# One transformer block with its gradients on one core: where the second layout of the MLP activation is made, how w2's gradient is laid out for its store, and who issues two small loads

## The chip, the cores and the metric

The kernel runs on one NeuronCore of a Trainium2 chip. The metric is the time of one execution in microseconds of device time; three executions of the kernel before were timed and their median is quoted. One more look, the profile, comes from a single profiled execution. Engine names as in the profile: PE (matrix products; PEld is its weight load), DVE (vector), ACT (scalar/activation), POOL (GpSimd), SP (issues transfers). Transfers are issued by SP, ACT or POOL and carried out by sixteen DMA engines.

## The reference

One decode step of a pre-layernorm block and all its gradients, in bfloat16, batch 2, one query position, width 640, 32 heads of 128, a cache of 4096 positions, MLP width 1728:

```
h   = x + attention(layernorm(x), k_cache, v_cache, wq, wo)     # 32 heads, 4096 keys each
h2  = h + relu(layernorm(h) @ w1) @ w2                          # 640 -> 1728 -> 640
out = h2, and for grad_out: the gradients of x, k_cache, v_cache, wq, wo, w1, w2
```

The caches are 67 MB each (2 x 32 x 4096 x 128 in two bytes), and so are their two gradients. The gradient of w2 is an outer product: for each of 1728 rows f and 640 columns d, the sum over the two batch items of relu(h1)[b, f] * grad_out[b, d]. It is output 7, 1728 x 640. The gradient of w1 is output 6, those of wo and wq outputs 5 and 4.

## The kernel before

**Stages.** The 64 pairs of batch item and head are handled twice. Phase 1 (`p1_iter`) loads the pair's K and V tiles (1 MB each), computes scores, softmax and the quantities for the output. Phase 2 (`p2_iter`) needs the gradient that comes back through the MLP and wo, reads V again where it was not kept (`Wt`, 53 loads), and stores the pair's gradients of K and V (`gK`, `gV`, 1 MB each, issued by POOL, lines 856 and 875). Between them, for each batch item, `middle_gen` (line 719) does the attention output, the second layernorm, the MLP, and the gradient back to the heads. Phase 2 of batch item 0 runs beside phase 1 of item 1.

**Order.** The order is written by hand. The plan loop (line 1116) walks the iterations, and after each piece of an iteration gives a share of steps to three lists of background generators: `bg` (middle_gen and what follows it, `mlp_out` last), `bg2` (`fin_gen`, line 933: the weight gradients) and `bg3` (`gx_gen`, the gradient of x). A generator yields a number that says how much of the share the step used, so taking out or adding steps moves everything the generator emits later against the main iterations. Each engine carries out what it is given in this order.

**Buffers.** The big tiles come from rings of buffers with the tags `ld` (loads), `g` (gK, gV), `f` (weight gradients) and `q`. A ring's buffer is free again when its last reader is through, which for a stored tile is when the store has landed. At the start of `fin_gen` ring `f` has one buffer (line 1145). Eight banks of PSUM are given out by role; the role `mid` has one bank, used by all small products.

**The MLP activation in two layouts.** relu(layernorm(h) @ w1) is wanted with the 1728 rows on partitions. `acol` has row c*128+p in partition p, place c (13 full places and one of 64 rows, NF = 14). For item 1, `middle_gen` also makes `arow`, which has row p*13+c in partition p, place c: lines 751 to 760, 65 products that take w1 as weights with every 13th column, then two small DVE copies. `arow` is read only by `mlp_out` (line 691), whose w2 tiles are loaded so that each partition's rows lie together in memory.

**The row form.** `rows_of` (line 882) turns a column form into rows: `ar` has the activation as a row of 1728 per batch item, in partitions q and q+1 for q = 0, 32, 64, 96; `gr` has grad_out likewise.

**w2's gradient.** `fin_gen` calls `outer_rows` (line 903) for it with cc = 1728 // 96 = 18, so that P = 96 partitions are used and partition p has rows p*18 to p*18+17. Six places go into one tile (`ot`): 6 x 2 products of depth two (512 and 128 columns), each followed by an ACT copy from PSUM to the tile (line 928), then one store issued by ACT (line 930). There are three such tiles, 720 KB each. The same function makes the other weight gradients with 128 partitions.

**The small loads.** x and grad_out (2.5 KB each) are the first two transfers that SP issues (lines 210, 211); the five tiles of wq (1 MB each, line 378) and then K and V tiles follow on the same queue.

Of the kernel before, what the change touches and what calls it, by code (L numbers as in the profile page):

```python
# [7 lines left out]
FP32 = mybir.dt.float32  # L8
# [7 lines left out]
def kernel(  # L16
# [56 lines left out]
    def pst(shape, dtype, role, name):  # L73

        k = banks[role].pop(0)
        banks[role].append(k)
        return ps.tile(shape, dtype, tag=f"bank{k}", bufs=1, name=name)
# [36 lines left out]
    def rested(tag, n):  # L114

        return free[tag] > 0 and (forced[0] or step[0] >= given_at.get(homes[tag][0], -n) + n)
# [90 lines left out]
    nc.vector.memset(acol[:], 0.0)  # L207
    nc.vector.memset(ghfc[:], 0.0)

    nc.sync.dma_start(out=xr[0:2 * ND, :], in_=A_x.rearrange("b s (c p) -> (b s c) p", p=128))  # L210
    nc.sync.dma_start(out=xr[2 * ND:4 * ND, :], in_=grad_out.rearrange("b s (c p) -> (b s c) p", p=128))


    def colsum(src, n):
# [504 lines left out]
    def middle_gen(b):  # L719
        if o_next[0] < (b + 1) * H // OG:  # L720
            o_group()
        nc.vector.tensor_reduce(out=u4[:], in_=u_bank[0][:].rearrange("p (s d) -> p d s", s=4),
                                axis=AX.X, op=ALU.add)
        yield
        while a_next[0] < (b + 1) * H // OG:
            if a_next[0] == o_next[0]:
                o_group()
                yield
                yield
            a_group()  # L730
            yield
        at_bf = small.tile([128, ND], BF16, tag="at_bf", bufs=1, name="at_bf")
        nc.vector.tensor_copy(out=at_bf[:], in_=asum[:, b, :])
        nc.vector.tensor_tensor(out=h1c[:, :, b], in0=xg32[:, b, :], in1=at_bf[:], op=ALU.add)
        h32 = small.tile([128, 1, ND], FP32, tag="h32", bufs=1, name="h32")
        nc.vector.tensor_copy(out=h32[:, 0, :], in_=h1c[:, :, b])
        yield ("a", b)
        u_out(b)
        yield from ln_fwd(h32[:], 1, x2c[:, :, b:b + 1], rstd2[:, b:b + 1])
        hf_ps = pst([128, NF], FP32, "mid", "hf_ps")  # L740
        for cf in range(NF):
            kc = f_kc(cf)
            for c in range(ND):
                nc.tensor.matmul(hf_ps[0:kc, cf:cf + 1], lhsT=w1_t[:, c, cf * 128:cf * 128 + kc],
                                 rhs=x2c[:, c, b:b + 1], start=(c == 0), stop=(c == ND - 1))
            yield 0.25
        nc.vector.tensor_scalar(out=acol[:, 0:NFF, b], in0=hf_ps[:, 0:NFF], scalar1=0.0, scalar2=None, op0=ALU.max)
        if F_rem:
            nc.vector.tensor_scalar(out=acol[0:F_rem, NFF, b:b + 1], in0=hf_ps[0:F_rem, NFF:NF],
                                    scalar1=0.0, scalar2=None, op0=ALU.max)  # L750
        if b == B - 1:
            ar_ps = pst([128, NFF, B], FP32, "mid", "ar_ps")
            for cf in range(NFF):
                for c in range(ND):
                    nc.tensor.matmul(ar_ps[:, cf, :], lhsT=w1_t[:, c, bass.ds(cf, 128, step=NFF)],
                                     rhs=x2c[:, c, :], start=(c == 0), stop=(c == ND - 1))
                yield 0.25
            nc.vector.tensor_scalar(out=arow[:, 0:NFF, :], in0=ar_ps[:], scalar1=0.0, scalar2=None, op0=ALU.max)
            if F_rem:
                nc.vector.tensor_copy(out=arow[:, NFF, :], in_=acol[:, NFF, :])  # L760
        mask = small.tile([128, NF], FP32, tag="mask", bufs=1, name="mask")
        nc.vector.tensor_single_scalar(out=mask[:], in_=acol[:, :, b], scalar=0.0, op=ALU.is_gt)
        nc.vector.tensor_tensor(out=ghfc[:, :, b], in0=ga[:, b, :], in1=mask[:], op=ALU.mult)
        yield from wait(3)
        fbc = cols.tile([128, Dff], BF16, tag="fbc", name="fbc")
        gx2 = small.tile([128, 1, ND], FP32, tag="gx2", bufs=1, name="gx2")
        gx2p = small.tile([128, ND, 3], FP32, tag="gx2p", bufs=1, name="gx2p")
        FW = Dff // 3
        spread_f = bcast_cols(one(ghfc, b), NF, f_kc, fbc)
        have = 0  # L770
        for k in range(3):
            while have < min(Dff, (k + 1) * FW):
                next(spread_f)
                have += 512
                yield
            for c in range(ND):
                yield from turn()
                ttr(w1_t[:, c, k * FW:(k + 1) * FW], fbc[:, k * FW:(k + 1) * FW], gx2p[:, c, k:k + 1], FW)
                yield 0.85
        nc.vector.reduce_sum(out=gx2[:, 0, :], in_=gx2p[:], axis=AX.X)  # L780
        yield ("w1", b)
        yield from ln_bwd(gx2[:], x2c[:, :, b:b + 1], rstd2[:, b:b + 1], gc[:, :, b:b + 1], gh1c[:, :, b:b + 1], 1)
        hbc = cols.tile([128, D], BF16, tag="rowbc", name="hbc")
        yield from bcast_cols(one(gh1c, b), ND, lambda c: 128, hbc)
        yield ("gh1", b)

        first = H - KEPT[b]
        bounds = [(first, first + 2), (first + 2, H)] if b == 0 else [(first, H)]
        bounds += [(h, min(first, h + GH)) for h in range(0, first, GH)]
        for h0, h1 in bounds:  # L790
            yield from go_group(b, h0, h1, hbc)
        if b > 0:
            yield from mlp_out()
# [106 lines left out]

    late = [False]

    def outer_rows(L, nrow, R, N, out_ap, cc):


        P = nrow // cc
        grp = max(1, min(cc, 4096 // N))
        out_v = out_ap.rearrange("(p c) n -> p c n", c=cc)
        for c0 in range(0, cc, grp):
            gn = min(grp, cc - c0)  # L910
            while not rested("f", 13):
                yield 0.0
            ot = take("f", [128, grp, N], "ot")
            todo = [(k, n0, min(512, N - n0)) for k in range(gn) for n0 in range(0, N, 512)]
            made = []
            for x in range(len(todo) + 1):
                if x < len(todo):
                    k, n0, nn = todo[x]
                    q = 32 * (fw[0] % 4)
                    o_ps = pst([128, 512], FP32, "o", "o_ps")  # L920
                    fw[0] += 1
                    nc.tensor.matmul(o_ps[0:P, 0:nn], lhsT=L[q:q + B, bass.ds(c0 + k, P, step=cc)],  # L922
                                     rhs=R[q:q + B, n0:n0 + nn], start=True, stop=True)
                    made.append((o_ps, k, n0, nn))
                    yield 0.3
                if x > 0:
                    o_ps, k, n0, nn = made[x - 1]
                    nc.scalar.copy(out=ot[0:P, k, n0:n0 + nn], in_=o_ps[0:P, 0:nn])  # L928
                    yield 0.3
            nc.scalar.dma_start(out=out_v[:, c0:c0 + gn, :], in_=ot[0:P, 0:gn, :])  # L930
            give(ot)

    def fin_gen(fin):
        FIN["wide"] = [fin.tile([128, 4, 4, 32], BF16, tag="wide", bufs=2, name="wide") for _ in range(2)]
        for w in FIN["wide"]:
            nc.vector.memset(w[:], 0.0)
        yield from wait(2)
        yield from rows_of(fin, acol, NF, "ar", "rX")
        yield from rows_of(fin, gc, ND, "gr", "rD")
        yield from outer_rows(FIN["ar"], Dff, FIN["gr"], D, out_7, Dff // 96)  # L940
        yield from rows_of(fin, ghfc, NF, "ghfr", "rX")
        yield from rows_of(fin, x2c, ND, "x2r", "rD")
        yield from outer_rows(FIN["x2r"], D, FIN["ghfr"], Dff, out_6, ND)
        HH = H // 2
        while ("gh1", B - 1) not in done:
            yield
        yield from rows_of(fin, gh1c, ND, "gh1r", "rD")
        for s0 in range(0, H, HH):
            yield from rows_of(fin, OFc[:, s0:s0 + HH, :], HH, "OFr", "rX")
            yield from outer_rows(FIN["OFr"], HH * 128, FIN["gh1r"], D, out_5[s0 * 128:(s0 + HH) * 128, :], HH)  # L950
        yield from rows_of(fin, x1c, ND, "x1r", "rD")
        for s0 in range(0, H, HH):
            while not all(("go", B - 1, h) in done for h in range(s0, s0 + HH)):
                yield
            yield from rows_of(fin, GQc[:, s0:s0 + HH, :], HH, "GQr", "rX")
            yield from outer_rows(FIN["x1r"], D, FIN["GQr"], HH * 128, out_4[:, s0 * 128:(s0 + HH) * 128], ND)
# [277 lines left out]
```

## Time and profile before

| what | value |
|---|---|
| time, three runs | 910.86, 903.35, 911.38 us; median 910.86 |
| span of the profiled execution | 905.5 us; no time of its own is given beside the span |
| busy: PE, DVE, ACT, POOL | 742.8, 696.1, 444.7, 192.4 us |
| moved by the DMA engines | 362.87 MB, mean 401 GB/s |
| the 65 products for arow (line 755) | from 499.3 to 506.8 us |
| first and last store of a weight gradient issued by ACT (line 930) | 583.7 and 870.8 us |

How to read it: the span runs from the first to the last instruction of the profiled execution. A busy time is the sum over an engine's instructions, and engines work side by side, so busy times do not add up to the span. The views split the span into windows and give, for each, the busy time of each engine with the number of instructions in brackets, the clock that was granted to PE (1.00 is full), the share of the sixteen DMA engines that was busy (1.00 is all of them all the time; pipelining lets it go slightly above) and the rate they moved.

### The profile page before, as it was taken

The numbers are of one execution on the slowest core, as the hardware profiler recorded it, in microseconds if no ns is written. First come the engines' busy times: TensorE is split into PE (matmuls) and PEld (weight loads), VectorE is DVE, ScalarE is ACT, GpSimd is POOL, SyncE is SP. The second block draws the span as 40 slices with busy tenths as digits, with TensorE's granted clock in tenths as the row PEclk, the third lists the DMA queues.
The fourth block names the chain that finished last, engine by engine and source line by source line (L and its number), as shares of the span: only waits on it lengthen the run. The fifth ranks groups of instructions, "written<-read, shape, count | busy, mean of one in ns | idle before, by whom it ended". The sixth has DMA issues, their size and how long they took to land.

```text
span 905.5 us, 24516 instructions
## 1 busy us (share of the span) xinstructions
PE 742.8 (82%) x10205; PEld 620.3 (68%) x10205; DVE 696.1 (77%) x1286; ACT 444.7 (49%) x1096; POOL 192.4 (21%) x330
## 2 busy tenths in 40 slices
PE   3999899899998997987968854877899879859880
PEld 3887788788887887876857744655667656645560
DVE  2666787777888796777869698986898349989982
ACT  1444343344554564554543434644576656637750
POOL 1344433443211110010011111211122111111120
PEclk9999999999999899999885776655555555555655
DMA  8999999999879999999999999999999999999997
GB/s 361 420 409 403 409 398 410 420 417 388 335 306 377 377 406 425 421 424 421 411 398 392 411 423 394 423 398 396 407 401 388 426 420 423 419 423 416 419 421 296
DMA packets 56254, 362.87 MB, mean 401 GB/s; under 512 B 5680, under 2 KB 11696, under 8 KB 15312
## 3 DMA queue, kind: packets, MB, share of 16 engines
q1 hardware_dynamic: 34704, 212.18, 58.1%
q0 software_dynamic: 18432, 134.23, 35.9%
q10 hardware_dynamic: 3008, 14.91, 4.2%
q8 instruction: 80, 1.31, 0.6%
q14 instruction: 30, 0.25, 0.1%
HBM read 212.16 MB, written 149.13 MB: 399 GB/s over the span
## 4 chain that ended last, share of the span: by engine, by line
PE 42%; DMA 25%; DVE 18%; issue 6%; ACT 6%; SPq 1%; POOL 0%; POOLq 0%; ACTq 0%; DVEq 0%
PE t_ps L423 18%; DMA Vt<-in_A_v_cache_dram 13%; PE m_ps L457 9%; DVE gV L818 5%; DMA out_dram<-gV 4%; DVE gK L818 4%; DMA out_dram<-gK 3%; PE s_ps L436 3%; ACT t_sb L428 3%; DMA wqs<-in_A_wq_dram 3%; DVE gxj L644 2%; PE u_ps L486 2%; PE o_ps L922 2%; PE dp_ps L436 2%; DVE pk L464 2%
## 5 line engine op out<-in xcount | busy, mean ns | idle before, releaser
L428 ACT COPY t_sb<-t_ps 128x512 f32<-128x512 f32 x479 | 274.4, 586 | 214.6 <-PE t_ps L423 208.9
L436 PEld LDWEIGHTS <-t_sb 128*128 128x128 bf16 x4096 | 179.0, 102 | 47.0 <-issue 18.8
L423 PE MATMUL t_ps<-ident_f,Wt 128*128 128x128 f32 x848 | 196.5, 379 | 0.2 <-ACT t_sb L428 0.2
L457 PE MATMUL m_ps<-pk,Vt 128*128 128x129 bf16 x2048 | 171.0, 222 | 19.5 <-DMA Vt<-in_A_v_cache_dram 18.2
L464 DVE TENSOR_TENSOR pk<-Kt,ep 128x2048 bf16<-128x2048 bf16 x128 | 156.5, 1223 | 33.9 <-PE m_ps L457 15.8
L818 DVE TENSOR_TENSOR gK<-rb,gsp 128x2048 bf16<-128x2048 bf16 x128 | 152.4, 1225 | 18.4 <-DMA out_dram<-gV 16.4
L818 DVE TENSOR_TENSOR gV<-rb,pp 128x2048 bf16<-128x2048 bf16 x128 | 153.0, 1219 | 15.1 <-DMA out_dram<-gK 12.5
L423 PE MATMUL t_ps<-ident_f,Kt 128*128 128x128 f32 x1024 | 155.1, 284 | 6.6 <-DMA Kt<-in_A_k_cache_dram 6.3
L423 PEld LDWEIGHTS t_ps<-ident_f,Wt 128*128 128x128 f32 x848 | 135.7, 196 | 35.1 <-issue 29.3
L457 PEld LDWEIGHTS <-Vt 128*128 128x128 bf16 x2048 | 124.5, 98 | 51.0 <-issue 29.7
L423 PEld LDWEIGHTS t_ps<-ident_f,Kt 128*128 128x128 f32 x1024 | 112.6, 144 | 10.9 <-PE s_ps L436 4.6
L474 POOL COPY pk<-ep 128x16 bf16<-128x16 bf16 x80 | 83.2, 1042 | 163.6 <-ACT ep L512 87.8
L436 PE MATMUL dp_ps<-gom,t_sb 128*128 128x2 bf16 x2048 | 95.6, 168 | 8.5 <-ACT t_sb L428 7.5
L875 POOL DMA_DIRECT2D out_dram<-gV x64 | 34.2, 534 | 268.0 <-DVE gV L818 207.7
L856 POOL DMA_DIRECT2D out_dram<-gK x64 | 34.0, 532 | 264.9 <-DVE gK L818 207.8
L436 PE MATMUL s_ps<-qm,t_sb 128*128 128x2 bf16 x2048 | 87.4, 164 | 1.5 <-DVE t_sb L426 1.5
L928 ACT CAST ot<-o_ps 128x512 bf16<-128x512 f32 (+4 forms) x160 | 70.4, 490 | 14.8 <-DMA out_dram<-ot 11.2
L571 ACT CAST MT<-m_ps 128x128 bf16<-128x128 f32 x64 | 17.1, 267 | 104.3 <-PE m_ps L457 104.2
L845 ACT ACTIVATE rb<-dp_ps,rt 128x256 bf16<-128x256 f32 x64 | 30.3, 474 | 69.4 <-PE dp_ps L840 68.7
L644 DVE CUSTOM_DVE_ANT_0 junk<-wo_t,hbc 128x640 bf16<-128x640 bf16 x64 | 52.4, 819 | 0.2
L644 DVE CUSTOM_DVE_ANT_0 gxj<-wqs,gqr 128x1024 bf16<-128x1024 bf16 x40 | 48.8, 1221 | 2.4 <-DMA wqs<-in_A_wq_dram 2.2
L831 DVE SCALAR_TENSOR_TENSOR gsp<-dp_ps,negdot,P_bf 128x64 bf16<-128x64 f32 x64 | 18.0, 281 | 42.3 <-PE dp_ps L436 42.0
(198 smaller groups left out, 719.5 us busy)
## 6 DMA issues: line engine op xcount, KB each, us to landing
Kt<-in_A_k_cache_dram SPq DMA_DIRECT2D x64, 1024.0 KB, 16.0
Vt<-in_A_v_cache_dram SPq DMA_DIRECT2D x64, 1024.0 KB, 15.9
out_dram<-gV POOLq DMA_DIRECT2D x64, 1024.0 KB, 14.7
out_dram<-gK POOLq DMA_DIRECT2D x64, 1024.0 KB, 14.4
Wt<-in_A_v_cache_dram SPq DMA_DIRECT2D x53, 1024.0 KB, 11.8
wq_t<-in_A_wq_dram SPq DMA_DIRECT2D x5, 1024.0 KB, 9.2
wo_t<-in_A_wo_dram SPq DMA_DIRECT2D x4, 1280.0 KB, 19.1
wqs<-in_A_wq_dram SPq DMA_DIRECT2D x5, 1024.0 KB, 17.1
```

The source lines that it names most:

```text
L423: nc.tensor.transpose(t_ps[:, j, :], natf[:, 2 * cc:2 * cc + 2, :].rearrange("p c k -> p (c k)"), ident_f[:])
L428: nc.scalar.copy(out=t_sb[:], in_=t_ps[:])
L436: nc.tensor.matmul(dst[:, sc:sc + 2], lhsT=v[:, j, :, par], rhs=vecs[:, par, :], start=(par == 0), stop=(par == 1))
L457: nc.tensor.matmul(r["m"][:, 0:129], lhsT=r["V"][:, sc, :], rhs=r["pk"][sc // HALF][:, sc % HALF, 0:129], start=(sc == 0), stop=(sc == NSC ...
L464: nc.vector.tensor_tensor(out=p["pk"][k][:, :, 0:128].rearrange("p s (a two) -> p s a two", two=2), in0=p["K"][:, sl, :].rearrange("p s (a ...
L474: nc.gpsimd.tensor_copy(out=col, in_=e)
L644: nc.vector.tensor_tensor_reduce(out=junk[0:kc, 0:width], in0=in0, in1=in1, scale=1.0, scalar=0.0, op0=ALU.mult, op1=ALU.add, accum_out=acc)
L818: nc.vector.tensor_tensor(out=pairs_view(dst[:, sl, :]), in0=row.rearrange("p (a two) -> p a two", two=2)[:, None, :, :].to_broadcast([128 ...
L845: nc.scalar.activation(out=rb[:], in_=bank[:, 128:384], func=ACT.Copy, scale=rt[:, b, h:h + 1])
L856: nc.gpsimd.dma_start(out=natural(out_2, bp, hp), in_=gK[:])
L875: nc.gpsimd.dma_start(out=natural(out_3, b, h), in_=gV[:])
L928: nc.scalar.copy(out=ot[0:P, k, n0:n0 + nn], in_=o_ps[0:P, 0:nn])
```

## The change

1. `arow` is no longer made in `middle_gen`. `fin_gen`, right after `ar` and `gr`, makes 13 products of depth two with slices of `ar` (every 13th element) as weights and a 2 x 2 identity, and two ACT copies bring the result into `arow`.
2. w2's gradient is made by a new function `w2_rows` with 128 partitions: partition p has rows p*13 to p*13+12, in tiles of 5, 4 and 4 places, and the last 64 rows go as a fifth place into the last tile with a store of their own. The body of `outer_rows` that fills a tile becomes `outer_tile`, used by both.
3. The loads of x and grad_out are issued by ACT.

```diff
-    nc.sync.dma_start(out=xr[0:2 * ND, :], in_=A_x.rearrange("b s (c p) -> (b s c) p", p=128))
-    nc.sync.dma_start(out=xr[2 * ND:4 * ND, :], in_=grad_out.rearrange("b s (c p) -> (b s c) p", p=128))
+    nc.scalar.dma_start(out=xr[0:2 * ND, :], in_=A_x.rearrange("b s (c p) -> (b s c) p", p=128))
+    nc.scalar.dma_start(out=xr[2 * ND:4 * ND, :], in_=grad_out.rearrange("b s (c p) -> (b s c) p", p=128))
...
-        if b == B - 1:
-            ar_ps = pst([128, NFF, B], FP32, "mid", "ar_ps")
-            for cf in range(NFF):
-                for c in range(ND):
-                    nc.tensor.matmul(ar_ps[:, cf, :], lhsT=w1_t[:, c, bass.ds(cf, 128, step=NFF)],
-                                     rhs=x2c[:, c, :], start=(c == 0), stop=(c == ND - 1))
-                yield 0.25
-            nc.vector.tensor_scalar(out=arow[:, 0:NFF, :], in0=ar_ps[:], scalar1=0.0, scalar2=None, op0=ALU.max)
-            if F_rem:
-                nc.vector.tensor_copy(out=arow[:, NFF, :], in_=acol[:, NFF, :])
...
+    def outer_tile(todo, L, R, ot, stores):
+        made = []
+        for x in range(len(todo) + 1):
+            if x < len(todo):
+                sl, P, k, n0, nn = todo[x]
+                q = 32 * (fw[0] % 4)
+                o_ps = pst([128, 512], FP32, "o", "o_ps")
+                fw[0] += 1
+                nc.tensor.matmul(o_ps[0:P, 0:nn], lhsT=L[q:q + B, sl], rhs=R[q:q + B, n0:n0 + nn],
+                                 start=True, stop=True)
+                made.append((o_ps, P, k, n0, nn))
+                yield 0.3
+            if x > 0:
+                o_ps, P, k, n0, nn = made[x - 1]
+                nc.scalar.copy(out=ot[0:P, k, n0:n0 + nn], in_=o_ps[0:P, 0:nn])
+                yield 0.3
+        for out_ap, src in stores:
+            nc.scalar.dma_start(out=out_ap, in_=src)
+        give(ot)
...
+    def w2_rows(L, R):
+        out_v = out_7[0:NFF * 128, :].rearrange("(p c) n -> p c n", c=NFF)
+        c0 = 0
+        for gn in (5, 4, 4):
+            while not rested("f", 13):
+                yield 0.0
+            ot = take("f", [128, 6, D], "ot")
+            last = c0 + gn == NFF
+            cs = [(bass.ds(c0 + k, 128, step=NFF), 128, k) for k in range(gn)]
+            if last and F_rem:
+                cs.append((slice(NFF * 128, Dff), F_rem, gn))
+            todo = [(sl, P, k, n0, min(512, D - n0)) for sl, P, k in cs for n0 in range(0, D, 512)]
+            stores = [(out_v[:, c0:c0 + gn, :], ot[:, 0:gn, :])]
+            if last and F_rem:
+                stores.append((out_7[NFF * 128:Dff, :], ot[0:F_rem, gn, :]))
+            yield from outer_tile(todo, L, R, ot, stores)
+            c0 += gn
...
-        yield from outer_rows(FIN["ar"], Dff, FIN["gr"], D, out_7, Dff // 96)
+        ar_ps = pst([128, NFF, B], FP32, "mid", "ar_ps")
+        for c in range(NFF):
+            nc.tensor.matmul(ar_ps[:, c, :], lhsT=FIN["ar"][0:B, bass.ds(c, 128, step=NFF)],
+                             rhs=ident_bf[0:B, 0:B], start=True, stop=True)
+        yield from wait(1)
+        nc.scalar.copy(out=arow[:, 0:NFF, :], in_=ar_ps[:])
+        if F_rem:
+            nc.scalar.copy(out=arow[:, NFF, :], in_=acol[:, NFF, :])
+        yield 0.5
+        yield from w2_rows(FIN["ar"], FIN["gr"])
```

In the order of the built program the loads of SP are the same but for two things: the two small loads are gone from its head, and one load of a `Wt` tile stands behind the first w2 tile of `mlp_out` instead of ahead of it.

More of the change, by code (lines that the diff above doesn't have):

```diff
@@ L913, in outer_rows @@
             ot = take("f", [128, grp, N], "ot")
[L914 to L931, printed above, removed]
+            todo = [(bass.ds(c0 + k, P, step=cc), P, k, n0, min(512, N - n0))
+                    for k in range(gn) for n0 in range(0, N, 512)]
+            yield from outer_tile(todo, L, R, ot, [(out_v[:, c0:c0 + gn, :], ot[0:P, 0:gn, :])])
+    def w2_rows(L, R):
[15 more added lines that the diff above has]
+            c0 += gn
     def fin_gen(fin):
```

## The prediction

> **What bounds the kernel now.** I read the rate of the DMA engines over the span first, since 362.87 MB in 905.5 us leaves little room. Each figure covers a fortieth of the span (22.6 us).
>
> ```profile
> DMA  8999999999879999999999999999999999999997
> GB/s 361 420 409 403 409 398 410 420 417 388 335 306 377 377 406 425 421 424 421 411 398 392 411 423 394 423 398 396 407 401 388 426 420 423 419 423 416 419 421 296
> ```
>
> The engines are full everywhere but at the start, in slices 11 and 12 (226 to 294 us, first batch item's middle) and at the end. At the best slice's 426 GB/s the bytes alone need 852 us; what is lost beyond that is idle time in those few places and slices that are full and yet carry less. A change saves time if it starts the stream sooner, raises the rate while the stream is full, or fills a hole. Next, the windows that the change touches, and what SP waits for.
>
> ```profile
> 498.00:512.00 14.00, 12.46 (x155) 11.75 (x156) 8.58 (x14) 4.61 (x9) 1.83 (x4) 0.52 1.00 412
> 512.00:584.00 72.00, 45.44 (x547) 37.55 (x547) 65.60 (x113) 35.94 (x78) 13.49 (x29) 0.73 1.01 413
> 584.00:640.00 56.00, 41.28 (x364) 33.07 (x362) 44.62 (x77) 27.23 (x59) 9.42 (x19) 0.53 1.01 400
> 640.00:706.00 66.00, 61.07 (x547) 47.66 (x547) 55.89 (x98) 44.14 (x100) 15.22 (x27) 0.53 0.99 399
> 706.00:880.00 174.00, 140.77 (x1216) 102.51 (x1216) 141.71 (x197) 104.01 (x222) 26.57 (x57) 0.54 1.01 421
> ```
>
> ```profile
> SPq L1229 <- DMA out_dram<-gV: 23.2, 1, 23.2
> ```
>
> The last two columns are the DMA share and GB/s. The share stays at 0.99 to 1.01 from 498 to 880 us, while PE, DVE and ACT all have idle time. The wait of SP at the program's end says the same: computing was over and 23.2 us were spent on stores already queued. Time that compute saves between 498 and 880 us only makes that queue longer. The chain of waits gives PE 42% and DMA 25% of the span; it names the last releaser of each step and does not contradict a full DMA stream beside it.
>
> **The change part by part.**
>
> *Small loads on ACT.* The timeline of SP and ACT at the start:
>
> ```profile
> 0.74 0.41 SPq L210 DMA_DIRECT2D xr<-in_A_x_dram  x1
> 1.21 0.29 SPq L211 DMA_DIRECT2D xr<-in_grad_out_dram  x1
> 1.54 2.07 SPq L378 DMA_DIRECT2D wq_t<-in_A_wq_dram  x4
> ```
>
> ```profile
> 0.74 1.28 ACT L428 ACT_TABLE_LOAD   x1 [0.74 <-PEq L1218]
> ```
>
> SP can issue the first wq tile at 0.74 instead of 1.54: 0.80 us sooner, and the stream is full from there until about 226 us. ACT issues the two loads ahead of its table load (two times the 0.3 to 0.4 us of its other issues); its first use of the table is at 21.36 us, so that is free. x can come later, since wq packets are now in the engines before it: it landed by 2.64 us and layernorm ends at 8.8 us, while the third wq tile lands only at 11.6, so about 2 us of lateness (after the 0.80) stay hidden. -0.80 us; bounds 0 (x late enough to eat it) and -0.80.
>
> *arow out of middle_gen.* Gone are 65 products and weight loads: on PE 0.77 + 1.02 + 1.36 + 1.35 = 4.50 us in the timeline from 499.3 to 506.8. DVE sat idle for them:
>
> ```profile
> 506.82 0.18 DVE L758 TENSOR_SCALAR arow<-ar_ps 128x26 bf16<-128x26 f32 x1 [5.35 <-PE ar_ps L755]
> ```
>
> So mask and ghfc, and the chain to gh1 and the heads of item 1, come some 5.4 + 0.3 us sooner, and the order shows two pairs' gK and gV work sliding behind them. The cover is the DMA share of 1.00 at 412 GB/s in just that window: taken at 0. Bounds: -5.7 us if the cover is a mistake; +0 on this side. What is late next for DVE is the store of the buffer it writes into (DVE waited 16.4 + 12.5 us in all for gV and gK stores to land), which is the DMA stream again.
>
> *arow from ar.* Added in fin_gen: 13 products of depth two with two columns. The nearest rows are those removed (0.068 us apart at 499 us) and mlp_out's products, 0.165 us each: 0.9 to 2.1 us of PE. Two ACT copies, nearest the copies to `wide` at 0.22 us and of a 128x128 block at 0.27: 0.5 us. Behind the first copy on ACT queue the t_sb copies of phase 2, for which PE waits; the copy waits for the products, already behind it by two steps. Covered by the same full stream (1.01): 0, bounds 0 and +2.6. mlp_out reads arow only from 739 us on, so nobody waits there. The products of w2's gradient fall from 36 to 28 and their copies likewise: 8 fewer, four of 0.58 and four of 0.27 us, -3.4 us of ACT; covered too, 0.
>
> *The stores from 128 partitions.* The first two stores each leave a mark. The windows are cut so that each store's packets lie in one (issue plus some 2 us to the landing):
>
> ```profile
> 574.00:584.00 10.00, 9.48 (x78) 7.30 (x78) 9.75 (x21) 5.40 (x13) 2.56 (x5) 0.50 1.01 425
> 586.00:594.00 8.00, 6.30 (x69) 5.62 (x68) 7.93 (x13) 3.85 (x7) 1.30 (x3) 0.71 1.02 359
> 594.00:612.00 18.00, 12.94 (x107) 10.16 (x107) 14.27 (x28) 8.69 (x21) 3.67 (x6) 0.50 1.01 418
> 612.00:622.00 10.00, 9.51 (x93) 8.28 (x91) 8.20 (x15) 4.90 (x9) 2.08 (x5) 0.50 1.02 373
> 622.00:636.00 14.00, 8.15 (x62) 6.06 (x59) 8.32 (x11) 5.95 (x15) 1.30 (x3) 0.50 1.01 417
> 640.00:646.00 6.00, 4.91 (x54) 4.66 (x54) 5.43 (x13) 3.19 (x8) 2.37 (x3) 0.50 1.00 402
> 706.00:716.00 10.00, 6.57 (x55) 5.29 (x55) 3.62 (x4) 5.98 (x12) 1.30 (x3) 0.50 1.01 426
> ```
>
> Against 418 GB/s between them, the first costs 8 x (1 - 359/418) = 1.13 us, the second 10 x (1 - 373/418) = 1.08, the third 6 x (1 - 402/418) = 0.23: 2.44 in all, at a share of 1.00 to 1.02, so the engines were slow, not idle. The last row holds the first store of wo's gradient, 128 partitions with runs of the same 7680 B: 426, no mark. With 128 partitions I expect that: -2.4 us; bounds 0 (the marks come from something else) and -2.4. The fourth store adds 64 rows of 1280 B. The nearest row with such runs is the stretch with the wo loads (20 to 225 us, 408 GB/s against 418): 82 KB at 408 rather than 418 is under 0.01 us; if it ran at a quarter of the engines it would be 0.8. Taken at +0.2, with one more issue of 0.35 us on ACT inside the cover.
>
> [...]
>
> *The two ACT waits.* Ring f has one buffer then, so the next tile's first copy waits for the store to land: 5.42 us at 592.3 and 5.74 at 620.7. This stays: tiles of 800, 640 and 720 KB (with the 64 rows) against three of 720. The landing took 14.0 us (583.7 to 597.7); in proportion to bytes the first wait becomes 7.0 and the second 4.2. Covered: 0. If the cover were gone, up to 11.2 us are in play.
>
> Sum: -0.80 - 2.4 + 0.2 + 0 = -3.0 us. The profiled execution (span 905.5) would become 902.5. The median of the runs, 910.86, lies 5.4 above that span and the lowest run 2.1 below it; the runs differ by more than the effect. On the median: 907.9.
>
> **The rivals.**
>
> *Compute was on the path after all.* For it: the chain's PE 42%, and PE at 61.07 of 66 us busy from 640 to 706 at a clock of 0.53. Against it: the share of 0.99 to 1.01. It would add the 5.7 us of the middle and perhaps half of the ACT waits (5.6): -14.3, 896.6 us.
>
> *The marks are not the 96 partitions.* For it: the third store left almost none, and 646 to 650 us, with no such store, ran at 395 GB/s. Then only the start is left: -0.8 + 0.2, 910.3 us.
>
> *Slower: the new order lets loads and stores hinder each other more.* Stretches exist that are full but carry less than the 421 of the late part: 450 to 480 at 398, 480 to 498 at 383, 640 to 706 at 399; they lose 30 x 23/421 + 18 x 38/421 + 66 x 22/421 = 6.7 us. Everything after 499 us is interleaved anew. If the loss came to three times that, +13.4 - 3.0 = +10.4, 921.3 us. It decides from 3.0 us lost; to be slower by over 1% it must lose 12.1. Against it: bytes, rings and the kinds of transfer stay the same.
>
> **How the numbers follow.** Forecast 0.64, marks elsewhere 0.16, compute on the path 0.12, slower order 0.08. About 1% (9.1 us) is what a measurement of this kernel can tell from no change. The runs before spread over 8.0 us, so with -3.0 a median that falls among the low ones (903.35 - 3.0 = 900.4) is over 1% faster; I give that an eighth of the forecast's chance: faster 0.08 + 0.12 = 0.20. Slower: 0.08, and 0.02 for a high median without a gain: 0.10. Same 0.70. The range goes from the first rival's nearer half, 898, to the slower order at half its price, 914.
>
> **What would show it.** Right: SP's first wq issue near 0.74 us; no ar_ps products near 500 us and no 5.35 us hole in DVE; 415 GB/s or more in the windows of the three w2 stores; SP's last wait still about 23 us. Wrong: the marks at 360 to 370 stay (second rival); the share falls under 0.97 between 500 and 880, or the last wait changes by over 5 us (then compute counts); full windows under 400 that were not there (third).

## The result and the profile after

| | before | after |
|---|---|---|
| median of the runs (us) | 910.39 (22 runs) | 904.24 (22 runs) |
| lowest to highest (us) | 903.35 to 916.85 | 899.89 to 910.55 |
| ratio to before, with its 95% interval | | 0.9945 [0.9927, 0.9962] |
| span of the profiled execution (us) | 905.5 | 901.1 |

The ratio is a gain of 5.0 us (3.5 to 6.6; the two medians differ by 6.15), against the 3.0 forecast: right in sign and place, too small by about two fifths. The page of the changed kernel still shows full DMA engines, except in slices 11 and 12 and at the end; the first slice now reads 9 instead of 8.

```profile
DMA  9999999999789999999999999999999999999997
GB/s 377 419 409 405 409 397 409 419 419 359 301 323 341 415 423 422 421 423 422 417 384 403 421 424 395 423 418 416 415 417 406 408 379 424 425 425 425 425 423 319
```

The next block has windows of the changed kernel, the same stretches as before and then the new w2 stores. Columns: window, length, busy time of PE, PE's weight loads, DVE, ACT and POOL (with instructions), granted clock, DMA share, GB/s. ACT issued the four stores at 576.72, 596.19, 617.93 and 618.94 us.

```profile
498.00:512.00 14.00, 12.13 (x126) 11.08 (x125) 11.48 (x21) 7.62 (x15) 2.90 (x7) 0.50 1.01 421
512.00:584.00 72.00, 50.95 (x545) 43.08 (x544) 65.84 (x113) 34.89 (x77) 12.82 (x29) 0.59 1.01 415
584.00:640.00 56.00, 37.77 (x357) 30.47 (x355) 44.87 (x80) 24.82 (x57) 9.48 (x20) 0.50 1.01 418
640.00:706.00 66.00, 54.13 (x517) 40.84 (x516) 53.88 (x87) 42.43 (x90) 14.71 (x27) 0.63 1.01 412
706.00:880.00 174.00, 143.31 (x1280) 104.96 (x1280) 144.15 (x199) 107.12 (x230) 28.61 (x59) 0.56 1.00 416
578.00:587.00 9.00, 6.58 (x91) 5.53 (x92) 8.93 (x15) 4.51 (x9) 1.83 (x4) 0.86 1.02 422
587.00:598.00 11.00, 7.39 (x60) 5.46 (x60) 8.62 (x17) 6.04 (x14) 2.50 (x5) 0.50 1.01 412
598.00:606.00 8.00, 7.20 (x84) 6.65 (x83) 5.28 (x12) 3.76 (x7) 1.31 (x3) 0.50 1.01 420
620.00:628.00 8.00, 2.10 (x27) 1.85 (x26) 6.46 (x11) 2.25 (x5) 1.31 (x3) 0.50 1.01 405
706.00:730.00 24.00, 20.21 (x180) 14.99 (x180) 9.48 (x11) 14.74 (x31) 2.38 (x6) 0.50 0.96 377
```

The marks are gone: 422 and 420 GB/s in the windows of the first two stores, where 359 and 373 stood. The window of the third, 620 to 628 us, has 405, below the 415 that the prediction named as a sign of being right; there the last 64 rows follow close behind. 584 to 640 us went from 400 to 418, 640 to 706 from 399 to 412. Some is given back: 706 to 730 us carries 377, where the kernel before had 424. The bytes that the trace's packets had moved by a given time put the changed kernel 0.2 us ahead at 584 us, 4.8 ahead at 706, 1.6 at 750 and 3.2 at 890.

The start, from the timelines of the changed kernel (start, duration, engine, line, operation, tiles; in brackets the idle time before it and what ended it):

```profile
0.74 2.64 SPq L378 DMA_DIRECT2D wq_t<-in_A_wq_dram  x5
0.75 0.62 ACTq L210 DMA_DIRECT2D xr<-in_A_x_dram  x1
1.40 0.30 ACTq L211 DMA_DIRECT2D xr<-in_grad_out_dram  x1
6.56 0.17 PE L315 MATMUL x_ps<-ident_bf,xr 20*128 20x20 bf16 x1 [6.56 <-DMA xr<-in_grad_out_dram]
12.80 4.43 PE L385 MATMUL q_ps<-x1c,wq_t 128*128 128x2 bf16 x160
```

SP's first wq issue is at 0.74 us, as forecast. The packets of the small loads now run among those of the 1 MB wq tiles, from 1.75 to 5.74 us instead of 1.72 to 2.21, so x is used at 6.56 us, where it was 2.67. The q products, which need it, still end earlier. Before, they ran in pieces, the last after a wait for its wq tile:

```profile
17.71 1.02 PE L385 MATMUL q_ps<-x1c,wq_t 128*128 128x2 bf16 x32 [2.57 <-DMA wq_t<-in_A_wq_dram]
```

Now all 160 run in one go, from 12.80 to 17.23 us; before, they ended at 18.73.

The middle, from DVE's timeline of the changed kernel:

```profile
499.35 0.17 DVE L747 TENSOR_SCALAR acol<-hf_ps 128x13 bf16<-128x13 f32 x1
499.43 0.14 DVE L749 TENSOR_SCALAR acol<-hf_ps 64x1 bf16<-64x1 f32 x1
499.60 0.17 DVE L752 TENSOR_SCALAR mask<-acol 128x14 f32<-128x14 bf16 x1
```

The 5.35 us hole is gone: mask follows acol at once. The end, from the waits of SP, and the waits of ACT for a w2 or later tile to land (total, times, longest), all of the changed kernel:

```profile
SPq L1253 <- DMA out_dram<-gV: 28.0, 1, 28.0
```

```profile
ACT ot L908 <- DMA out_dram<-ot: 9.2, 3, 5.2
```

SP's last wait grew from 23.2 to 28.0 us, where the prediction had it stay at about 23. It goes with the part on arow: 27.6 us in e3 below, with that part alone, 24.1 in e2 without it. That the computing saved became a longer queue of stores is the likely reading, not a shown one: in e9 and e7, where the same computing is done twice and four times, the wait did not get shorter (23.1 and 23.4).

### The profile page after: what moved, and what is told of

Same layout as the page of the kernel before. It is cut to its first block, busy times and chain, and to the rows that moved or that the text cites. A ratio compares the mean times of both kernels' runs of the same rounds, so it can differ in the third digit from the quotient of the medians.

```text
span 901.1 us, 24395 instructions
## 1 busy us (share of the span) xinstructions
PE 739.2 (82%) x10145; PEld 618.0 (69%) x10145; DVE 695.8 (77%) x1284; ACT 442.9 (49%) x1090; POOL 192.9 (21%) x330
## 3 DMA queue, kind: packets, MB, share of 16 engines
q8 instruction: 80, 1.31, 0.6%
## 4 chain that ended last, share of the span: by engine, by line
PE 47%; DMA 25%; DVE 15%; ACT 5%; issue 5%; SPq 0%; POOL 0%; ACTq 0%; POOLq 0%; DVEq 0%
PE t_ps L423 20%; DMA Vt<-in_A_v_cache_dram 12%; PE m_ps L457 10%; DMA out_dram<-gV 7%; DVE gV L808 5%; DMA out_dram<-gK 4%; PE s_ps L436 3%; DVE gK L808 3%; PE u_ps L486 3%; ACT t_sb L428 3%; PE o_ps L902 3%; PE dp_ps L436 2%; DVE pk L464 2%; DVE junk L644 2%; DMA Kt<-in_A_k_cache_dram 2%
## 5 line engine op out<-in xcount | busy, mean ns | idle before, releaser
L457 PE MATMUL m_ps<-pk,Vt 128*128 128x129 bf16 x2048 | 173.5, 224 | 18.0 <-DMA Vt<-in_A_v_cache_dram 16.0
L457 PEld LDWEIGHTS <-Vt 128*128 128x128 bf16 x2048 | 126.7, 99 | 49.2 <-issue 29.8
L423 PEld LDWEIGHTS t_ps<-ident_f,Wt 128*128 128x128 f32 x848 | 137.2, 198 | 29.3 <-issue 23.4
L908 ACT CAST ot<-o_ps 128x512 bf16<-128x512 f32 (+3 forms) x152 | 67.2, 492 | 10.7 <-DMA out_dram<-ot 9.2
## 6 DMA issues: line engine op xcount, KB each, us to landing
out_dram<-gV POOLq DMA_DIRECT2D x64, 1024.0 KB, 14.8
```

The source lines that it names most:

```text
L423: nc.tensor.transpose(t_ps[:, j, :], natf[:, 2 * cc:2 * cc + 2, :].rearrange("p c k -> p (c k)"), ident_f[:])
L457: nc.tensor.matmul(r["m"][:, 0:129], lhsT=r["V"][:, sc, :], rhs=r["pk"][sc // HALF][:, sc % HALF, 0:129], start=(sc == 0), stop=(sc == NSC ...
```

## The experiments

Theory A: the stream of transfers sets the time; the gain is the 96-partition stores (they slow the engines for everybody) plus the earlier start; the middle is covered. Rival B: the gain is compute, the 65 products out of the middle. Rival C: the marks have nothing to do with 96 partitions, but with the number of stores, the address pattern, or any store below 128 partitions. Ratios are to the kernel before, run on the same chip.

### e1: the two small loads on ACT, alone

```diff
-    nc.sync.dma_start(out=xr[0:2 * ND, :], ...)          # and the second
+    nc.scalar.dma_start(out=xr[0:2 * ND, :], ...)        # and the second
```

> Only the third part: the kernel before with the loads of x and grad_out issued by ACT. Stream theory (the full stream of transfers sets the time, each part is worth what it adds to that stream): first wq issue at 0.74 us, some 0.8 us ahead in bytes at 200 us, -0.8 us, ratio about 0.999, too small to see in the times; windows of w2's three stores still at 360 to 400 GB/s. Compute theory (part of the gain of the change is compute time saved in the middle): the same, as this part saves no compute. Third theory (the new order of loads and stores): a change of the order at the start alone should move nothing later.

909.9 us, 0.9985 [0.9961, 1.0008]. The windows of e1 that hold its three w2 stores:

```profile
587.00:598.00 11.00, 4.96 (x70) 4.14 (x69) 10.90 (x19) 3.75 (x7) 2.08 (x5) 0.91 1.00 365
614.00:627.00 13.00, 6.48 (x87) 5.75 (x86) 8.61 (x15) 3.99 (x8) 2.08 (x5) 0.76 1.01 367
642.00:653.00 11.00, 8.77 (x89) 8.08 (x90) 7.98 (x19) 6.23 (x15) 2.91 (x5) 0.50 1.01 383
```

The marks stay; against 418 GB/s they cost 1.39 + 1.59 + 0.92 = 3.9 us. Each window holds the whole store, whose packets ran from 588.5 to 596.2, 615.9 to 625.2 and 643.7 to 651.0 us. In bytes moved, e1 is 0.8 to 0.9 us ahead of before from 10 to 200 us, the 0.80 of the prediction. Whether that arrives at the end is below what these runs resolve.

### e2: the 128-partition stores alone

```diff
-        yield from outer_rows(FIN["ar"], Dff, FIN["gr"], D, out_7, Dff // 96)
+        yield from w2_rows(FIN["ar"], FIN["gr"])
```

with `w2_rows` and `outer_tile` of the change; arow still comes from w1 in the middle.

> Only the second part: w2's gradient from 128 partitions, arow still made in the middle from w1, SP issues the small loads. Stream theory: the marks of the three stores are gone (415 GB/s or more against 359, 373, 402), -2 to -3 us, ratio 0.997 to 0.998. Compute theory: the 8 fewer products and copies and shorter waits of ACT count as well, -3 to -6 us. If the marks are not from the 96 partitions: they stay, ratio 1.000.

903.08 us, 0.9936 [0.9913, 0.9959]: 5.8 us (3.7 to 7.9). The windows of e2's three large w2 stores:

```profile
586.00:594.00 8.00, 5.24 (x83) 4.51 (x80) 7.93 (x12) 3.91 (x8) 1.39 (x4) 0.90 1.02 427
607.00:614.00 7.00, 6.34 (x66) 5.63 (x65) 6.65 (x17) 3.40 (x6) 2.37 (x3) 0.50 1.02 427
626.00:636.00 10.00, 5.03 (x48) 4.36 (x46) 6.41 (x9) 4.20 (x11) 1.30 (x3) 0.50 1.02 415
```

No marks, and this part alone gives a gain that agrees with that of the whole change. As a size it is not what theory A expected (2 to 3 us lies below the interval) but what the compute theory did (3 to 6 us): e2 also has 8 fewer products and copies, and these were not tried apart from the stores. Its one profiled execution has a span of 906.8 us, longer than that of before: in bytes moved it was already some 4 us behind at 584 us (see the last section), so a single span would have hidden the result.

### e3: arow from its row form alone

```diff
-        if b == B - 1:
-            ar_ps = pst([128, NFF, B], FP32, "mid", "ar_ps")
...
+        ar_ps = pst([128, NFF, B], FP32, "mid", "ar_ps")
+        for c in range(NFF):
+            nc.tensor.matmul(ar_ps[:, c, :], lhsT=FIN["ar"][0:B, bass.ds(c, 128, step=NFF)],
+                             rhs=ident_bf[0:B, 0:B], start=True, stop=True)
...
         yield from outer_rows(FIN["ar"], Dff, FIN["gr"], D, out_7, Dff // 96)
```

> Only the first part: arow from the row form, w2's gradient still from 96 partitions, SP issues the small loads. Stream theory: 0 us, ratio 1.000, the 5.35 us hole of DVE near 500 us is gone and SP's last wait is longer by that much at most; the windows of the three stores keep their marks (two of three under 380 GB/s). Compute theory: -3 to -6 us, ratio 0.994 to 0.997.

909.74 us, 0.9988 [0.9964, 1.0012]: -1.1 us (-3.3 to +1.1). The windows of e3's stores, and those between them:

```profile
584.00:593.00 9.00, 6.82 (x76) 5.64 (x75) 8.88 (x16) 3.99 (x7) 1.83 (x4) 0.69 1.00 368
593.00:609.00 16.00, 13.55 (x113) 10.63 (x113) 11.14 (x23) 9.18 (x21) 2.08 (x5) 0.50 1.01 420
609.00:618.00 9.00, 6.31 (x77) 5.41 (x75) 6.73 (x11) 3.40 (x6) 1.31 (x3) 0.69 1.01 360
618.00:636.00 18.00, 12.67 (x99) 9.90 (x99) 16.20 (x32) 9.09 (x22) 4.20 (x7) 0.50 1.01 420
636.00:647.00 11.00, 9.62 (x132) 7.88 (x130) 6.23 (x9) 9.08 (x22) 1.78 (x3) 0.79 1.01 351
```

All three stores leave a mark here, 1.08 + 1.25 + 1.76 = 4.09 us, and between them the rate is 420. The hole of DVE is gone and the time did not fall with it: B, which needed 3 to 6 us from this part, falls for the change as made, but for the very edge of the interval.

### e4: both, without the ACT loads

The change without its first hunk.

> The first and second part, SP issues the small loads as before. Stream theory: the whole change without its 0.8 us at the start, ratio 0.995 to 0.998, marks gone. Compute theory: ratio 0.993 to 0.996, nearly all of the change's gain. If the start is worth more than 0.8 us, this loses more than 1 us against the changed kernel.

903.52 us, 0.9924 [0.9901, 0.9946]: 6.9 us (4.9 to 9.0). Not slower than the whole change; the 0.8 us cannot be seen in times. Theory A's range, 0.995 to 0.998, is missed here as in e2: the gain is larger.

### e5 and e6: every weight-gradient store cut in 96 + 32, or 64 + 64 partitions

In `outer_tile` of the changed kernel, for the 18 stores of 128 partitions (the last one, of 64 rows, is left whole):

```diff
-            nc.scalar.dma_start(out=out_ap, in_=src)
...                                                       # the 64-row store as before
+            for p0, p1 in ((0, 96), (96, 128)):          # e6: ((0, 64), (64, 128))
+                nc.scalar.dma_start(out=out_ap[p0:p1], in_=src[p0:p1])
```

> The changed kernel, but each of the 18 weight-gradient stores from 128 partitions is issued as two, partitions 0 to 95 and 96 to 127; addresses, bytes and all computing stay. If the shape of 96 partitions makes the marks: every such store gets one, 14.8 MB against the 2.2 MB of before; a mark cost 1.0 to 1.8 us for 0.74 MB in three profiles, so +15 to +30 us against the changed kernel, 920 us or more, and 4096-byte and 6912-byte packets above their 160 and 262 ns too. If the address pattern of 18 rows per partition makes them: no marks, since the addresses are those of the changed kernel; only 17 more issues of 0.35 us on ACT, 904 to 907 us.

> The same with a cut at 64: two stores of 64 partitions each. [...] Address theory: no marks.

e5: 928.77 us, 1.022 [1.0183, 1.0258]; e6: 928.19 us, 1.0202 [1.0166, 1.0238]. Over the changed kernel that is about 25 and 23 us (1.022 and 1.0202 over 0.9945, of 904 us) for the same bytes. One line of each, the window from 584 to 820 us that the experiments are compared by below, e5 and then e6:

```profile
584.00:820.00 236.00, 173.19 (x1590) 132.70 (x1588) 171.90 (x267) 123.93 (x276) 35.98 (x75) 0.54 1.00 388
```

```profile
584.00:820.00 236.00, 174.07 (x1640) 134.11 (x1639) 177.36 (x276) 126.56 (x281) 38.38 (x76) 0.57 1.00 382
```

The share is still 1.00, at 388 and 382 GB/s where the changed kernel has 414: slow engines, not idle ones, as at the marks of before. The page's lines of the DMA queues say whose packets are slow (packets, MB, share of 16 engines' time over the span; q1 carries SP's loads, q0 the stores of gK and gV that POOL issues, q10 ACT's stores). The changed kernel, e5, e6:

```profile
q1 hardware_dynamic: 34664, 212.17, 58.3%
q0 software_dynamic: 18432, 134.23, 35.7%
q10 hardware_dynamic: 3224, 14.92, 4.0%
```

```profile
q1 hardware_dynamic: 34664, 212.17, 56.9%
q0 software_dynamic: 18432, 134.23, 36.3%
q10 hardware_dynamic: 3512, 14.92, 5.2%
```

```profile
q1 hardware_dynamic: 34664, 212.17, 57.0%
q0 software_dynamic: 18432, 134.23, 35.4%
q10 hardware_dynamic: 3512, 14.92, 5.8%
```

Times the spans (901.1, 924.9, 929.4 us), ACT's stores went from 36.0 us of all engines to 48.1 in e5 and 53.9 in e6; POOL's stores from 321.7 to 335.7 and 329.0; the loads from 525.3 to 526.3 and 529.8. In e5 the cut stores themselves thus account for some 12 us and what runs beside them for some 15; in e6 for 18 and 12.

### e8: as many stores as in e5 and e6, cut by places

```diff
-            nc.scalar.dma_start(out=out_ap, in_=src)
...                                                       # the 64-row store as before
+            for ks, ns in parts:                         # halves of the places; of the columns where there is one place
+                nc.scalar.dma_start(out=out_ap[:, ks, ns], in_=src[:, ks, ns])
```

> Control for the two split kernels: the changed kernel with each of the 18 weight-gradient stores issued as two, but cut by places, so that each half still comes from all 128 partitions (18 more issues of 0.35 us on ACT, runs half as long). If the number of stores cost the 24 us of the two splits: about 928 us here too. If reaching only part of the partitions did: no marks, 903 to 908 us, 5120 to 7680 byte packets gone and their halves at 26 GB/s per engine.

903.47 us, 0.9926 [0.989, 0.9962]. 36 stores instead of 18, each of 128 partitions, cost nothing: the number of stores is out.

### e10: 64 + 64 again, even and odd partitions

```diff
-            nc.scalar.dma_start(out=out_ap, in_=src)
...                                                       # the 64-row store as before
+            for p0 in (0, 1):
+                nc.scalar.dma_start(out=out_ap[bass.ds(p0, 64, step=2)], in_=src[bass.ds(p0, 64, step=2)])
```

> The changed kernel with each of the 18 weight-gradient stores cut into the even and the odd partitions, 64 each. Cutting at 64 and at 96 had cost some 24 us against the changed kernel, cutting by places nothing. [...]

906.36 us, 0.996 [0.9928, 0.9992]. Two stores of 64 partitions each, as in e6, without e6's 23 us. So it is not "fewer than 128 partitions", nor the count: which partitions a store takes decides. One thing changes along with them: a store of e6 writes into one half of the output, one of e10 into the whole, the rows of every second partition. No run holds one of the two and changes the other. Against the addresses speaks that the slow stores of the kernel before run over the whole gradient, as the fast ones of e10 do. Nor do the traces say which of the sixteen engines carried which partitions. ACT's queue in e10, and its window from 584 to 820 us:

```profile
q10 hardware_dynamic: 3512, 14.92, 4.0%
```

```profile
584.00:820.00 236.00, 185.83 (x1677) 140.69 (x1673) 182.47 (x282) 132.73 (x294) 37.88 (x78) 0.54 0.99 401
```

As many packets as in e6, and they take 4.0% of the engines' time against e6's 5.8. A packet of 6912 B takes a mean of 460 ns in e6, 352 in e5, 267 in e10 and 268 in the changed kernel. So the 401 GB/s, below the changed kernel's 414, are not slow stores; in part they are idle time, above all from 706 to 730 us (share 0.90, 347 GB/s), a stretch that comes up again below.

In the time of ACT's own packets 64 + 64 costs more than 96 + 32 (17.9 us more than in the changed kernel against 12.1), in the time of the kernel the two cost the same. Why partitions 0 to 95 and 0 to 63 in a row are slow and every second one is not, no run shows.

### e9 and e7: the 65 products done twice and four times

In the kernel before:

```diff
-            for cf in range(NFF):
+            for again in range(2):                       # e7: range(4)
+                for cf in range(NFF):
...
-                yield 0.25
+                    yield 0.125                          # e7: 0.0625
```

> The kernel before with the 65 products for arow done four times over in the middle (the result is the same); some 13.5 us more of PE near 500 us. Stream theory: the transfers issued ahead cover it, 0 to +3 us, ratio 1.000 to 1.003; SP's last wait gets shorter by up to 13 us; the DMA share in the windows after 500 us falls below 0.97 only if the cover is used up. Compute theory: +10 to +16 us, ratio 1.011 to 1.018.

> The kernel before with the 65 products for arow done twice. Done four times, DVE's hole grew from 5.35 to 16.63 us (3.76 us for each further time) and the time by 8.9 to 14.6 us: the cover by transfers issued ahead ran out. Cover theory: it covers the hole of 5.35 us and little more, some 7 to 8 us, so here a hole of 9.1 us costs 1 to 2 us and the DMA share dips in the 14 us after 512 us, to 0.85 to 0.95 instead of 0.45. If every us of hole counted (no cover): +3.8 us here, the dip as deep as the hole is longer, and the 65 products taken out would have given 5 us.

e7: 921.71 us, 1.0129 [1.0098, 1.0161], +11.7 us (8.9 to 14.6); e9: 913.18 us, 1.0027 [0.9993, 1.0061]. A's expectation for e7 (0 to +3) is missed, B's is met. The e9 times (-0.6 to +5.5 us) fit both the 1 to 2 us of a cover and the 3.8 of none; what the DMA engines do tells more. DVE's timeline shows the hole, and the windows show what the transfers do in it. e7:

```profile
522.82 0.19 DVE L759 TENSOR_SCALAR arow<-ar_ps 128x26 bf16<-128x26 f32 x1 [16.63 <-PE ar_ps L756]
```

```profile
498.00:512.00 14.00, 9.81 (x150) 9.53 (x149) 7.87 (x10) 1.57 (x4) 3.09 (x6) 0.50 1.01 423
512.00:526.00 14.00, 14.00 (x205) 13.60 (x204) 3.11 (x8) 2.76 (x5) 0.00 (x0) 0.50 0.45 170
526.00:540.00 14.00, 11.57 (x175) 9.90 (x173) 12.54 (x19) 10.01 (x19) 2.61 (x6) 0.94 0.90 333
```

and e9:

```profile
516.37 0.18 DVE L759 TENSOR_SCALAR arow<-ar_ps 128x26 bf16<-128x26 f32 x1 [9.15 <-PE ar_ps L756]
```

```profile
512.00:526.00 14.00, 12.58 (x177) 11.34 (x176) 8.53 (x14) 6.99 (x13) 1.31 (x3) 0.71 0.88 322
```

The share falls only after the hole has lasted a while. e7: 14 x 0.55 + 14 x 0.10 = 9.1 us idle for a hole of 16.63; e9: 14 x 0.12 = 1.7 for 9.15. The difference is 7.5 us both times: about so much of a hole the transfers already queued cover. The hole of before, 5.35 us, ended some 2 us short of that, and e3, which takes it away, gained nothing clear. "Covered" was true, and no more than just.

## Why the prediction was right, and which term was too small

*What bounds the kernel.* Right. e5 and e6, which slow a full stream and leave the computing as it is, lose some 25 and 23 us, and e3, which takes 5.35 us off DVE under a full stream, gains nothing clear. The two slices that are not full end at 272 us, not at 294.

*Small loads on ACT, -0.80.* The first issue came at 0.74, the lead in bytes is 0.8 to 0.9 us. The allowance was off: "about 2 us of lateness" hidden, and x came 3.9 us later. It stayed hidden since the last wq tile, not x, had set the end of the q products. Whether the 0.80 arrives at the end, no run shows.

*arow out of middle_gen, 0.* Right (e3, -3.3 to +1.1), by a margin of some 2 us (e7, e9). The bound of -5.7 did not come true.

*arow from ar, 0.* 13 products in 0.88 us and copies of 0.19 and 0.20 us, within the 0.9 to 2.1 and 0.5 given; mlp_out reads arow from 726 us on.

*The stores from 128 partitions, -2.4: the mis-sized term.* It was measured on one profile, and with windows that end before the stores do. The first store landed at 597.7 us, its window ended at 594; the third store's packets ran to 648.0, so the 395 GB/s from 646 to 650 us, which the second rival takes for a stretch without such a store, belong in part to its mark. Windows of the kernel before from ahead of each store's first packet to its end:

```profile
586.00:598.00 12.00, 6.30 (x69) 5.62 (x68) 9.89 (x17) 4.15 (x8) 2.08 (x5) 0.64 1.01 375
614.00:627.00 13.00, 7.60 (x77) 6.76 (x76) 8.95 (x14) 4.16 (x9) 1.36 (x4) 0.50 1.01 376
640.00:650.00 10.00, 8.10 (x87) 7.40 (x87) 8.24 (x18) 5.24 (x14) 3.14 (x5) 0.50 1.01 399
```

Against the same 418 GB/s that is 1.23 + 1.31 + 0.45 = 3.0 us, more than the bound of 2.4. e1 and e3 issue the same three stores, and theirs come to 3.9 and 4.1; the mean is 3.7. The packets, one by one, agree. The first 288 packets of 7680 B that ACT's queue stores are w2's, from 96 partitions, the 512 later ones come from 128: in the kernel before they took a mean of 384 ns against 293 (e1 410, e3 434, e7 383 and e9 375, against 291 or 292). All packets of ACT's and POOL's stores together took 361.6 to 362.6 us of the sixteen engines in these five kernels, and 358.0 to 359.2 in the five without such stores (after, e2, e4, e8, e10): some 3.5 us. With 3.5 the sum is -0.8 - 3.5 + 0.2 = -4.1, inside the interval of the change (-6.6 to -3.5).

That does not explain all of it. Without the 0.8 the sum is 3.3 us, and e2 gained 5.8 (3.7 to 7.9), e4 6.9 (4.9 to 9.0). The rest, 2.5 and 3.6 us by the middle of these intervals, 0.4 and 1.6 at their lower ends, was not found. The 8 fewer products and copies and the shorter waits of ACT, in both, stand as an untested rival for it.

*What one store of 96 partitions costs.* The marks say 1.2 us (3.7 / 3). Its own packets pay about half of it: w2's 288 packets were slower than the later ones by 1.5 to 2.6 us of sixteen engines in the five profiles, 0.5 to 0.9 a store. The rest is paid by what shares the engines: POOL's 8192 B packets took a mean of 318 ns from 584 us on in the kernel before, against 314 in the changed kernel, and 337 in e5. Per 0.74 MB e5 pays 1.2 us (25 us for 14.8 MB), though a part of its stores takes 32 partitions.

*The 64-row store, +0.2.* Its packets ran from 626.0 to 630.6 us; 625 to 631 us ran at 403, 6 x (1 - 403/418) = 0.2. It fits, but the end of the third large store lies in that window too; it was not tried alone.

*The two ACT waits, 7.0 and 4.2, covered.* They became:

```profile
589.52 0.59 ACT L908 CAST ot<-o_ps 128x512 bf16<-128x512 f32 x1 [5.23 <-DMA out_dram<-ot]
...
608.94 0.75 ACT L908 CAST ot<-o_ps 128x512 bf16<-128x512 f32 x2 [1.80 <-DMA out_dram<-ot]
```

Scaling with the bytes was the error: the first tile is larger and yet landed 12.8 us after its issue (576.72 to 589.52) instead of 14.0. That the waits are covered was not tried alone.

*The rivals.* "Compute on the path" fell with e3, but e7 shows that it waits close by. "Marks not the 96 partitions" fell: e2 alone removes them, e1 and e3 keep them, e5 slows ACT's packets at the same size (352 ns against 268 for 6912 B), and e8 and e10 exclude count and size. "Slower order" is there in small: 706 to 730 us runs at 377 GB/s in the changed kernel, 368 in e4, 381 in e8 and 347 in e10 (shares 0.90 to 0.97), and at 424 to 426 in before, e1, e2, e7 and e9. It comes where arow and the stores are both changed (though e6, which has both, runs at 421 there), and 24 x (1 - 377/424) = 2.7 us is its price, against the 13.4 of the rival. Taken into the sum it leaves 1.4 of the 4.1 us, so the account by parts falls short of the measured 5.0; the profile's lead in bytes, 3.2 us at 890, lies between. Its cause was not settled. SP's last wait changed by 4.8 us, just inside the 5 that the prediction allowed.

No experiment beat the change for certain: e2, e4 and e8 have 0.9936, 0.9924 and 0.9926, all with intervals that overlap its own.

## What to carry to other kernels

Where the transfers are full and yet carry less, cut windows around single transfers: here a share of 1.01 at 375 GB/s came with slow packets (384 ns against 293, the kernel before), a share of 0.45 at 170 GB/s with engines that stood idle (e7). Let each window hold all of the transfer's packets, up to its landing, and size such a mark on several profiles before it goes into a sum: the same three stores showed 2.4 us in windows cut short, and 3.0, 3.9 and 4.1 in whole ones. And a stall that is covered has a margin, here some 2 us: lengthen it on purpose, twice and four times, to learn how much is left.

## What was not expected of the hardware

- Stores of 64 partitions in a row (0 to 63, 64 to 127), in a full stream, cost about 1.2 us per 0.74 MB (e6: 23 us for 14.8 MB); the same number of partitions taken every second one cost nothing that could be measured (e10: 0.996 of the kernel before, the change 0.9945).
- The cover of queued transfers in the middle was some 7.5 us in two kernels alike (e7, e9).
- From 225 to 300 us profiles differ though no edit touches that stretch: e1 carried 337 GB/s, e2 333, e9 320, e4 346 and before 348. 348 against 320 is 6 us, from one profile each. It may be a large part of the 10 us by which runs of one kernel differ; that was not tried, and its cause stays open. So does why the third mark was 0.45 us in one profile and 1.76 in another.
